# The opening of a fused DFT and gated feed-forward kernel: x laid out at partitions 0-46 and 64-110, its reversed halves loaded through ScalarE's queue, and the weight folds moved

## The chip, the cores and the metric

The program runs on one core of a Trainium2 chip. The metric is device microseconds from the start to the end of one execution. The profile is that of one more execution, with its own time; stamps count from the start of its span.

## What is computed

The reference takes x, eight sequences of 3008 tokens with 256 values each, and makes a two-dimensional Fourier transform of each (over the tokens and over the values), of which it keeps the real part. Each of the 24064 rows then goes through a small feed-forward layer: it is multiplied by a 256 x 2048 matrix, the result h becomes h cos(h), and that is multiplied by a 2048 x 256 matrix. All is float32.

```python
X = np.fft.fft(x, axis=1)
X = np.fft.fft(X, axis=2)
x = X.real.reshape(B * S, D)
h = x @ w_in
g = h * np.cos(h)
return g @ w_out
```

## The kernel before

The transform over 3008 = 47 x 64 tokens is split in two. A **first half** multiplies rows of x by a constant matrix L (the 47-point part); its result z goes through a scratch in DRAM, which changes the order of its axes, and comes back as z2. A **second half** multiplies z2 by the constants BJ (the 64-point part with the twiddle factors) and gives pq. The transform over the 256 values is never made by itself: it is folded into the first weight, WC and WS, by multiplying the constants CS with w_in (`weights`, L408) in four quarters of 512 columns. One row of each folded quarter is also turned into a column (`weight_row`, L428, then wn on ScalarE and a memset of that row on GpSimd, L442). `fold_quarter(n)` does all of this for a quarter: four matmuls of 512 columns, each in two passes, two copies from PSUM by ScalarE and the row.

Symmetry halves the work. Sequence index i (0 to 31) is paired with 64 - i, so x is loaded twice over: 47 rows forward and 47 rows with the index running backward. In the kernel before they lie at partitions 0-46 and 47-93 of a tile "xp". A tile holds eight values of i (a piece p of 0 to 3), and a piece is loaded by four transfers (six for p = 0): 32 rows and 15 rows, forward (L147) and reversed (L155; for p = 0 L150 and L151). The forward rows are 8 KB in one run each; the reversed ones are runs of 1 KB. For the first sequence (b = 0) VectorE folds the two halves of the 256 values together (`fold`, L227), while GpSimd copies two edge columns (L234); a chunk is half a piece, so there are eight chunks. Two buffers xf0 take the chunks in turn, so the fold of chunk c + 2 waits until TensorE has read chunk c. TensorE's `first_half` (L250 to L267) makes z of a chunk, ScalarE copies it out of PSUM (L279), and `store_z` (L317) and `load_z` (L327) take it through DRAM.

The order of every engine's instructions is written out by hand: instructions run on their engine in the order in which the program names them (`manual_schedule`). All DMAs but two at the very end are issued by SP (SyncE). DMAs take eight landing semaphores in turn. The order of the opening stands at L191 to L195 and L746 to L833: L, piece 0 of x, CS, weight quarter 0, piece 1; chunks 0 to 2, quarter 0 folded, two stores of z; weight quarter 1, pieces 2 and 3; chunks 3 and 4, quarter 1 folded, and so on; after chunk 7 the first part of z (columns of j 0 to 3) goes out and comes back while quarter 2 is folded and six passes of filler matmuls run (`keep_busy(3, "M", 256)`, L464); then come the later parts of z, quarter 3, w2, and the second half for the first group. The main loop, eight sequences by six groups by eight steps, follows at L835, and works on later sequences' first halves between its own matmuls.

Of the kernel before, what the change touches and what calls it, by code (L numbers as in the profile page):

```python
# [18 lines left out]
ND = 256  # L19
NDFF = 2048  # L20
N2 = 47
NJ = 24
NI = 32
IP = 4
# [8 lines left out]
def _consts():  # L33

    s2 = np.arange(N2)
    j = np.arange(NJ)
    th = 2.0 * np.pi * np.outer(s2, j) / N2
    thm = 2.0 * np.pi * np.outer(46 - s2, j) / N2  # L40
    thh = 2.0 * np.pi * np.outer(s2 + 0.5, j) / N2
    z = np.zeros((N2, NJ))
    pad = np.zeros((2 * N2, 16))

    def stack(a, b, c, d):
        m = np.block([[a, b], [c, d]]).reshape(2 * N2, 2, NJ).transpose(0, 2, 1)
        return np.concatenate([m.reshape(2 * N2, 2 * NJ), pad], axis=1)

    LE = stack(np.cos(th), -np.sin(th), np.cos(thm), -np.sin(thm))
    LO = stack(np.sin(th), np.cos(th), -np.sin(thm), -np.cos(thm))  # L50
    LE0 = stack(np.cos(th), z, z, np.cos(thh))
    LO0 = stack(np.sin(th), z, z, np.sin(thh))
    L = np.concatenate([LE, LO, LE0, LO0], axis=1)
    L = np.concatenate([L, np.zeros((128 - 2 * N2, 256))], axis=0)

    k2 = np.arange(64)
    i = np.arange(NI)
    B = np.zeros((128, NJ, 128))
    for jj in range(NJ):
        phi = 2.0 * np.pi * np.outer(i, 47 * k2 + jj) / SEQ  # L60
        blk = np.concatenate([np.cos(phi), np.sin(phi)], axis=0)
        blk[0] = 1.0
        blk[NI] = np.where(k2 % 2 == 0, 1.0, -1.0)
        blk = blk.reshape(2, 2, 16, 64)
        for half in range(2):
            for r in range(2):
                for e in range(2):
                    p = 64 * half + 32 * r + 16 * e
                    B[p : p + 16, jj, 64 * e : 64 * e + 64] = blk[r, half]

    c = np.arange(ND)
    d = np.arange(128)
    ang = 2.0 * np.pi * np.outer(c, d) / ND
    CS = np.concatenate([np.cos(ang), -np.sin(ang)], axis=1) / TWO_PI
    CS[:, 128] = np.where(c % 2 == 0, 1.0, -1.0) / TWO_PI
    return (
        L.astype(np.float32),
        B.reshape(128, NJ * 128).astype(np.float32),
        CS.astype(np.float32),
    )  # L80
# [28 lines left out]
def kernel(  # L109
# [22 lines left out]
    ctx.enter_context(tc.manual_schedule())  # L132


    xs = {}

    def take_x(b, p):
        xs[b, p] = spool.tile([128, XP * ND], FP, tag="xp", bufs=4, name="xp")

    def load_x(b, p):  # L140
        if (b, p) not in xs:
            take_x(b, p)
        xt = xs[b, p]
        xv = xt.rearrange("r (i d) -> r i d", d=ND)
        i0 = XP * p
        for r0, r1 in ((0, 32), (32, 47)):
            nc.sync.dma_start(out=xv[r0:r1], in_=x_r[b, r0:r1, i0 : i0 + XP, :])  # L147
            q0, q1 = N2 + r0, N2 + r1
            if p == 0:
                nc.sync.dma_start(out=xv[q0:q1, 0:1], in_=x_r[b, r0:r1, 32:33, :])  # L150
                nc.sync.dma_start(  # L151
                    out=xv[q0:q1, 1:XP], in_=x_r[b, r0:r1, 63 : 64 - XP : -1, :]
                )
            else:
                nc.sync.dma_start(  # L155
                    out=xv[q0:q1], in_=x_r[b, r0:r1, 64 - i0 : 64 - i0 - XP : -1, :]
                )

# [26 lines left out]
    def load_w2(f0, f1):  # L185
# [2 lines left out]
            in_=moe_w_out.rearrange("(q p) c -> p q c", p=128)[:, 2 * f0 : 2 * f1],  # L188
        )

    nc.sync.dma_start(out=L, in_=L_dr.ap())  # L191
    load_x(0, 0)
    load_cs()
    load_w(0)
    load_x(0, 1)  # L195
    WC = cpool.tile([128, NDFF], FP, tag="WC", name="WC")
    WS = cpool.tile([128, NDFF], FP, tag="WS", name="WS")
    wn = cpool.tile([128, 16], FP, tag="wn", name="wn")
# [19 lines left out]

    def fold(b, c, e):
        lo = IP * (c % 2)  # L220
        xv = xs[b, c // 2].rearrange("r (i d) -> r i d", d=ND)[0 : 2 * N2, lo : lo + IP]
        if b == 0:
            xfs[b, c] = xf0[c % 2]
        elif e == 0:
            xfs[b, c] = spool.tile([128, 2 * IP * 128], FP, tag="xf", bufs=2, name="xf")
        fv = xfs[b, c].rearrange("r (e i d) -> r e i d", e=2, d=128)[0 : 2 * N2]
        (nc.gpsimd if b else nc.vector).tensor_tensor(  # L227
            out=fv[:, e, :, 1:128],
            in0=xv[:, :, 1:128],
            in1=xv[:, :, 255:128:-1],  # L230
            op=ALU.subtract if e else ALU.add,
        )
        if e:
            (nc.scalar.copy if b else nc.gpsimd.tensor_copy)(  # L234
                out=fv[:, :, :, 0].rearrange("r e i -> r i e"), in_=xv[:, :, 0:129:128]
            )
# [2 lines left out]

    def first_half(b, c, pz=None):  # L240

        rows = 2 * N2 if b else 128
        fv = xfs.pop((b, c)).rearrange("r (e c) -> r e c", e=2)[0:rows]
        LE, LO, LE0, LO0 = (L[0:rows, 64 * q : 64 * q + 64] for q in range(4))
        pz = pz or psum("pz", "M")
        a = 128 if c == 0 else 0
        for e, (w, w0) in enumerate(((LE, LE0), (LO, LO0))):
            rows = slice(64 * e, 64 * e + 64)
            if a:
                nc.tensor.matmul(  # L250
                    pz[rows, 0:128], lhsT=w0, rhs=fv[:, e, 0:128], start=True, stop=True
                )
            nc.tensor.matmul(  # L253
                pz[rows, a:512],
                lhsT=w,
                rhs=fv[:, e, a:512],
                start=not a,
                stop=True,
                skip_group_check=True,
            )  # L260
        if b:
            return pz
        if a:
            nc.tensor.matmul(
                pz[64:128, 0:1], lhsT=LE0, rhs=fv[:, 1, 0:1], start=True, stop=True
            )
        nc.tensor.matmul(  # L267
            pz[64:128, a:512:128],
            lhsT=LE,
            rhs=fv[:, 1, a:512:128],  # L270
            start=True,
            stop=True,
        )
        keep_z(b, c, pz)
# [10 lines left out]
    zm = cpool.tile([128, NI], FP, tag="zm", name="zm")  # L285

    def take_middle(b, p):
        xv = xs[b, p].rearrange("r (i d) -> r i d", d=ND)[0 : 2 * N2]
        nc.scalar.copy(out=xm[0 : 2 * N2, XP * p : XP * p + XP], in_=xv[:, :, 128])

    def clear_middle():
        pm = borrow("pm", 1)[64:128, 0:NI]
# [3 lines left out]
    def middle(pm):  # L296
        for i0, i1, q in ((0, 1, 2), (1, NI, 0)):
            nc.tensor.matmul(  # L298
                pm[:, i0:i1],
                lhsT=L[0 : 2 * N2, 64 * q : 64 * q + 64],  # L300
                rhs=xm[0 : 2 * N2, i0:i1],
                start=False,
                stop=True,
                skip_group_check=True,
            )
# [1 line left out]
    zds = {}  # L307
    z2s = {}

    def store_z(b, c, j0=0, j1=NJ):  # L310
        half, q = divmod(c, NCH // 2)
        if q == 0 and j0 == 0:
            zds[b, half] = dpool.tile([32, 2 * NJ * 128], FP, tag="zd", bufs=4, name="zd")
        zd, zs = zds[b, half], zss[b, c]
        for e in range(2):
            p0 = 16 * e + IP * q
            nc.sync.dma_start(  # L317
                out=zd[p0 : p0 + IP, 256 * j0 : 256 * j1].rearrange("i (y d) -> y i d", d=128),
                in_=zs[64 * e + 2 * j0 : 64 * e + 2 * j1, :].rearrange("y (i d) -> y i d", d=128),
            )  # L320

    def load_z(b, half, j0=0, j1=NJ):
        if b not in z2s:
            z2s[b] = spool.tile([128, NJ * 128], FP, tag="z2", bufs=1, name="z2")
        for r in range(2):
            p0 = 64 * half + 32 * r
            nc.sync.dma_start(  # L327
                out=z2s[b][p0 : p0 + 32, 128 * j0 : 128 * j1].rearrange("i (j d) -> i j d", d=128),
                in_=zds[b, half].rearrange("i (j r d) -> r i j d", r=2, d=128)[r, :, j0:j1],
            )  # L330
# [123 lines left out]
    ones = cpool.tile([1, 128], FP, tag="ones", name="ones")  # L454
    nc.vector.memset(VX[:, 0:512], 1.0)
    nc.vector.memset(ones, 1.0)
    wrow = cpool.tile([1, 256], FP, tag="wrow", name="wrow")
    scratch = cpool.tile([1, 128], FP, tag="scratch", name="scratch")
    nc.scalar.activation(out=scratch, in_=ones, func=AF.Sin, bias=0.0, scale=SIN_SCALE / 8)
# [285 lines left out]

    keep_busy(2, "H", 512)  # L746
    keep_busy(2, "H", 512)
    chunk(0)
    chunk(1)
    first_half(0, 0)  # L750
# [4 lines left out]
    take_wn(0)  # L755
    store_z(0, 0, 0, 4)
    store_z(0, 1, 0, 4)
    load_w(1)
    load_x(0, 2)
    load_x(0, 3)  # L760
    chunk(3)
    first_half(0, 2)
    chunk(4)
    first_half(0, 3)
    fold_quarter(1)
    store_z(0, 2, 0, 4)
    store_z(0, 3, 0, 4)
    x1 = spool.tile([128, XP * ND], FP, tag="xp", bufs=4, name="wr")
    wr.append([x1[:, 1024 * i : 1024 * i + 1024] for i in range(2)])
    load_w(2)  # L770
    load_bj(0, 512)
    store_z(0, 0, 4)
    store_z(0, 1, 4)
    chunk(5)
    first_half(0, 4)
    chunk(6)
    first_half(0, 5)
    store_z(0, 4, 0, 4)
    store_z(0, 5, 0, 4)
    chunk(7)  # L780
    first_half(0, 6)
    first_half(0, 7)
    store_z(0, 6, 0, 4)
    store_z(0, 7, 0, 4)
    for half in range(2):
        load_z(0, half, 0, 4)
    fold_quarter(2)
    keep_busy(3, "M", 256)
    load_w(3)
    load_w2(0, 2)  # L790
    load_w2(2, 4)
    for c in range(2, 8):
        store_z(0, c, 4)
    load_bj(512, 1024)
    for half in range(2):
# [154 lines left out]
```

## Time and profile before

| what | us |
|---|---|
| median of the 3 runs shown | 1958.27 |
| lowest and highest of these | 1957.38, 1958.48 |
| the profiled execution's own time | 1957.18 |
| its span | 1955.4 |
| PE busy | 1940.8 |
| ScalarE (ACT), VectorE (DVE), GpSimd (POOL) busy | 1516.3, 1455.8, 1396.4 |

Landmarks of the opening, from the trace:

| event | us from the start of the span |
|---|---|
| filler matmuls at the start end | 7.58 |
| last transfer of piece 0 of x lands | 8.22 |
| first matmul of chunk 0 | 9.13 |
| weight quarter 0 has landed | 10.43 |
| piece 1 of x has landed | 14.73 |
| first matmul of chunk 2 | 16.54 |
| weight quarter 1 has landed | 18.85 |
| pieces 2 and 3 of x have landed | 22.47, 25.66 |
| matmuls of chunk 7 end | 29.45 |
| first part of z is back | 34.63 |
| first matmul of the second half (L341) | 35.38 |
| first matmul of the main loop (L517) | 37.26 |

How to read it: the page gives each engine's busy time; the chain of waits goes back from the last instruction to what released each one; the timeline lists instructions in order of time, with the start, the duration, the engine, the line, the tiles written and read, and in brackets the idle time before. An issue of a DMA appears under SPq or ACTq; the landing comes from the semaphore records. A matmul of float32 appears as two passes. The clock granted to TensorE stood at 0.999 of full in the mean.

### The profile page before, as it was taken

How to read it: one execution, taken by the hardware profiler on the slowest of the kernel's cores; microseconds unless marked ns; L12 is line 12 of the kernel's file. 1: busy time of each engine (PE TensorE's matmuls, PEld its weight loads, DVE VectorE, ACT ScalarE, POOL GpSimd, SP SyncE). 2: the span in 40 equal slices, each digit the busy share in tenths (PEclk: the TensorE clock that was granted, in tenths of full speed). 3: DMA queues.
4: the chain of work that ended last, by engine and by line, in shares of the span. 5: the costliest groups of instructions: out<-in, count | busy, mean ns of one | idle time of the engine just before them, and what ended most of it. 6: DMA issues, size and time to landing. Idle time of an engine off the chain costs nothing.

```text
span 1955.4 us, 29697 instructions
## 1 busy us (share of the span) xinstructions
PE 1940.8 (99%) x9262; PEld 1686.2 (86%) x9262; DVE 1455.8 (74%) x2529; ACT 1516.3 (78%) x3450; POOL 1396.4 (71%) x1593
## 2 busy tenths in 40 slices
PE   9999999999999999999999999999999999999998
PEld 4888888888988889888898888988889888898887
DVE  3767777777777777777777777777777777788886
ACT  3777778777787787877778787788777877778775
POOL 3777767787577876787667776687767777666775
PEclk9999999999999999999999999999999999999999
DMA  8511124011230223201241111411114111100001
GB/s 199 126 32 39 23 54 78 21 36 39 49 68 18 41 41 64 47 22 40 41 80 29 38 28 41 86 24 41 27 36 86 23 38 28 38 22 16 12 16 28
DMA packets 176690, 88.70 MB, mean 45 GB/s; under 512 B 103303, under 2 KB 173622, under 8 KB 174902
## 3 DMA queue, kind: packets, MB, share of 16 engines
q1 hardware_dynamic: 176374, 86.68, 21.5%
q8 instruction: 75, 1.23, 0.3%
q14 instruction: 81, 0.66, 0.1%
q10 hardware_dynamic: 160, 0.13, 0.0%
HBM read 49.50 MB, written 37.27 MB: 44 GB/s over the span
## 4 chain that ended last, share of the span: by engine, by line
PE 97%; DMA 1%; ACT 0%; DVE 0%; SPq 0%; issue 0%; POOL 0%; POOLq 0%; ACTq 0%
PE M L608 58%; PE H L517 33%; PE pz L253 3%; PE pb L341 2%; DMA xp<-in_x_dram 1%; PE pw L408 0%; DMA wr<-in_moe_w_in_dram 0%; DMA nb<-nd 0%; DMA nd<-pq 0%; PE pz L250 0%; PE pm L298 0%; PE pd L464 0%; DVE r L549 0%; ACT H L498 0%; ACT r L555 0%
## 5 line engine op out<-in xcount | busy, mean ns | idle before, releaser
L575 POOL TENSOR_TENSOR S<-r 128x512 f32<-128x512 f32 (+1 forms) x383 | 474.8, 1240 | 453.0 <-DVE r L559 408.1
L555 ACT ACTIVATE r<-r 128x512 f32<-128x512 f32 (+1 forms) x768 | 477.5, 622 | 257.4 <-DVE r L549 254.5
L549 DVE SCALAR_TENSOR_TENSOR r<-r,H 128x512 f32<-128x512 f32 (+1 forms) x768 | 518.9, 676 | 199.0 <-ACT r L545 174.6
L559 DVE SCALAR_TENSOR_TENSOR r<-H,r 128x512 f32<-128x512 f32 (+1 forms) x768 | 519.2, 676 | 132.5 <-ACT r L555 92.5
L608 PE MATMUL M<-S,VX 128*128 128x256 f32 (+1 forms) x2304 | 615.7, 376 | 0.0
L608 PEld LDWEIGHTS M<-S,VX 128*128 128x128 f32 x2304 | 435.8, 190 | 70.9 <-issue 22.7
L517 PE MATMUL H<-pq,WC 128*128 128x256 f32 (+1 forms) x1536 | 455.7, 378 | 3.1 <-ACT H L498 2.9
L517 PE MATMUL H<-pq,WS 128*128 128x256 f32 (+1 forms) x1536 | 451.5, 376 | 0.0
L545 ACT ACTIVATE r<-H 128x512 f32<-128x512 f32 (+1 forms) x768 | 447.6, 583 | 0.0
L533 DVE TENSOR_TENSOR H<-ew,H 128x256 f32<-128x256 f32 (+1 forms) x768 | 324.8, 423 | 140.5 <-PE H L517 81.6
L608 PE MATMUL M<-r,w 128*128 128x256 f32 (+1 forms) x1536 | 387.8, 375 | 0.0
L498 ACT ACTIVATE H<-nb,wn 128x256 f32<-128x256 f32 (+1 forms) x766 | 365.8, 478 | 2.7 <-DMA nb<-nd 1.3
L529 ACT ACTIVATE ew<-H 128x256 f32<-128x256 f32 (+1 forms) x768 | 287.3, 374 | 98.2 <-PE H L517 94.4
L608 PEld LDWEIGHTS M<-r,w 128*128 128x128 f32 x1536 | 300.4, 197 | 27.0
L517 PEld LDWEIGHTS H<-pq,WC 128*128 128x128 f32 x1536 | 279.3, 190 | 50.1 <-ACT H L498 18.0
L517 PEld LDWEIGHTS H<-pq,WS 128*128 128x128 f32 x1536 | 290.2, 190 | 33.3 <-ACT ew L529 1.1
L581 POOL TENSOR_TENSOR S<-S,r 128x256 f32<-128x256 f32 (+1 forms) x383 | 275.5, 719 | 30.0
L582 POOL TENSOR_TENSOR S<-r,S 128x256 f32<-128x256 f32 (+1 forms) x383 | 274.5, 717 | 30.0
L608 PE MATMUL M<-S,w 128*128 128x256 f32 (+1 forms) x768 | 225.4, 375 | 0.0
L608 PE MATMUL M<-r,VX 128*128 128x256 f32 (+1 forms) x768 | 225.4, 375 | 0.0
L608 PEld LDWEIGHTS M<-S,w 128*128 128x128 f32 x768 | 150.6, 196 | 14.5
L608 PEld LDWEIGHTS M<-r,VX 128*128 128x128 f32 x768 | 146.0, 190 | 14.4
(74 smaller groups left out, 925.9 us busy)
## 6 DMA issues: line engine op xcount, KB each, us to landing
out_dram<-ob SPq DMA_DIRECT2D x728, 32.0 KB
xp<-in_x_dram SPq DMA_DIRECT2D x56, 256.0 KB
zd<-zs SPq DMA_DIRECT2D x112, 96.0 KB
z<-zd SPq DMA_DIRECT2D x28, 384.0 KB
xp<-in_x_dram SPq DMA_DIRECT2D x56, 120.0 KB
nb<-nd SPq DMA_DIRECT2D x40, 128.0 KB
wr<-in_moe_w_in_dram SPq DMA_DIRECT2D x8, 256.0 KB
w<-in_moe_w_out_dram SPq DMA_DIRECT2D x4, 512.0 KB
```

What stands on the lines that cost most here:

```text
L498: nc.scalar.activation(out=h.H[:, 0:T], in_=s.nb[:, 0:T], func=AF.Copy, bias=0.25, scale=wn[:, f : f + 1])
L517: nc.tensor.matmul(h.H[:, 0:T], lhsT=W[:, 128 * f : 128 * f + 128], rhs=s.pq[:, e * T : e * T + T], start=False, stop=True, skip_group_che ...
L529: nc.scalar.mul(out=h.ew[:, 0:T], in_=h.H[:, 0:T], mul=2.0)
L533: nc.vector.tensor_tensor(out=h.H[:, T : 2 * T][:, ::-1], in0=h.ew[:, 0:T], in1=h.H[:, 0:T], op=ALU.subtract)
L545: nc.scalar.activation(out=r, in_=y, func=AF.Copy, bias=BIG, scale=1.0)
L549: nc.vector.scalar_tensor_tensor(out=r, in0=r, scalar=-BIG, in1=y, op0=ALU.add, op1=ALU.subtract)
L555: nc.scalar.activation(out=r, in_=r, func=AF.Sin, bias=0.0, scale=SIN_SCALE)
L559: nc.vector.scalar_tensor_tensor(out=r, in0=y, scalar=-0.25, in1=r, op0=ALU.add, op1=ALU.mult)
L575: tt(out=sv[:, 0:2], in0=qv[:, 1:2].to_broadcast([128, 2, T]), in1=qv[:, 0:4:3], op=ALU.subtract,)
L581: tt(out=sv[:, 2], in0=sv[:, 1], in1=gv[:, 0, 0], op=ALU.subtract)
L582: tt(out=sv[:, 3], in0=gv[:, 1, 0], in1=sv[:, 2], op=ALU.add)
L608: nc.tensor.matmul(acc[key][m // 2][:, 256 * (m % 2) : 256 * (m % 2) + T], lhsT=w, rhs=a, start=first, stop=s.fp == 7, skip_group_check=True,)
```

## The change

Rows of x now lie at partitions 0-46 and 64-110 of one fixed tile for each piece, and L has its rows moved to match. The gap between them must hold zeros, so each tile gets one memset of partitions 32 to 63, by GpSimd for pieces 0 and 2 and by VectorE for 1 and 3; the transfer of rows 32 to 46 comes behind it. Operands of later sequences have 111 partitions instead of 94. For the first sequence the reversed rows are issued by ScalarE, the forward ones by SP; for later ones all by SP.

The order of the opening changes: the first transfer of x goes ahead of L; pieces 1 to 3 follow directly behind weight quarter 0; quarters 1 and 2 and a part of BJ come after all of x. Chunks 3 to 7 follow each other without a weight quarter between them. Quarters 1 and 2 are folded after chunk 7, where quarter 2 and the filler stood. Half 0 of z is loaded once chunks 0 to 5 have been sent to the store, half 1 after chunk 7; of the last store and the last load one transfer each is issued by ScalarE. The later parts of z of chunks 0 and 1 join those of the others, behind w2. Quarters 2 and 3 of the weight lie in two "r" buffers instead of an "xp" buffer.

```diff
-    L = np.concatenate([L, np.zeros((128 - 2 * N2, 256))], axis=0)
+    pad = [np.zeros((n, 256)) for n in (XO - N2, 128 - XR)]
+    L = np.concatenate([L[:N2], pad[0], L[N2:], pad[1]], axis=0)
...
+    xs = [cpool.tile([128, XP * ND], FP, tag=f"xp{p}", name=f"xp{p}") for p in range(4)]
+
+    def clear_gap(eng, p):
+        eng.memset(xs[p][32:XO], 0.0)
+
+    def load_x(b, p, parts=(0, 1)):
+        xv = xs[p].rearrange("r (i d) -> r i d", d=ND)
         i0 = XP * p
-        for r0, r1 in ((0, 32), (32, 47)):
+        back = nc.sync if b else nc.scalar
+        for r0, r1 in [((0, 32), (32, 47))[i] for i in parts]:
             nc.sync.dma_start(out=xv[r0:r1], in_=x_r[b, r0:r1, i0 : i0 + XP, :])
-            q0, q1 = N2 + r0, N2 + r1
+            q0, q1 = XO + r0, XO + r1
             if p == 0:
-                nc.sync.dma_start(out=xv[q0:q1, 0:1], in_=x_r[b, r0:r1, 32:33, :])
+                back.dma_start(out=xv[q0:q1, 0:1], in_=x_r[b, r0:r1, 32:33, :])
...
+    load_x(0, 0, (0,))
     nc.sync.dma_start(out=L, in_=L_dr.ap())
-    load_x(0, 0)
+    clear_gap(nc.gpsimd, 0)
+    load_x(0, 0, (1,))
     load_cs()
     load_w(0)
-    load_x(0, 1)
...
     nc.vector.memset(VX[:, 0:512], 1.0)
     nc.vector.memset(ones, 1.0)
+    for p in (1, 2, 3):
+        clear_gap(nc.gpsimd if p == 2 else nc.vector, p)
+        load_x(0, p)
...
     keep_busy(2, "H", 512)
     keep_busy(2, "H", 512)
+    load_w(1)
+    load_bj(0, 512)
+    wr.append([spool.tile([128, 1024], FP, tag="r", bufs=4, name="wr") for i in range(2)])
+    load_w(2)
     chunk(0)
...
-    load_w(1)
-    load_x(0, 2)
-    load_x(0, 3)
     chunk(3)
     first_half(0, 2)
     chunk(4)
     first_half(0, 3)
-    fold_quarter(1)
     store_z(0, 2, 0, 4)
     store_z(0, 3, 0, 4)
-    x1 = spool.tile([128, XP * ND], FP, tag="xp", bufs=4, name="wr")
-    wr.append([x1[:, 1024 * i : 1024 * i + 1024] for i in range(2)])
-    load_w(2)
-    load_bj(0, 512)
-    store_z(0, 0, 4)
-    store_z(0, 1, 4)
...
     store_z(0, 5, 0, 4)
+    load_z(0, 0, 0, 4)
     chunk(7)
     first_half(0, 6)
+    store_z(0, 6, 0, 4)
     first_half(0, 7)
-    store_z(0, 6, 0, 4)
-    store_z(0, 7, 0, 4)
-    for half in range(2):
-        load_z(0, half, 0, 4)
+    store_z(0, 7, 0, 4, True)
+    load_z(0, 1, 0, 4, True)
+    fold_quarter(1)
     fold_quarter(2)
-    keep_busy(3, "M", 256)
     load_w(3)
     load_w2(0, 2)
     load_w2(2, 4)
-    for c in range(2, 8):
+    for c in range(8):
         store_z(0, c, 4)
```

The scratch activation that brings in the table of the sine (L459) stands behind the loop over pieces 1 to 3 in the order of ScalarE.

## The prediction

> **What bounds it now.** I read the page first, its chain of work that ended last:
>
> ```profile
> PE 97%; DMA 1%; ACT 0%; DVE 0%; SPq 0%; issue 0%; POOL 0%; POOLq 0%; ACTq 0%
> ```
>
> TensorE carries nearly the whole span. PE is busy 1940.8 of 1955.4 us, and the main loop has no room that this edit touches: what can change is the opening, before the loop's first matmul at 37.26. So next the chain of waits for 0 to 36 us:
>
> ```profile
> 3.52 4.70 DMA xp<-in_x_dram
> ...
> 8.37 0.72 POOL xf L234
> 9.13 0.43 PE pz L250 x2
> ...
> 13.71 5.15 DMA wr<-in_moe_w_in_dram
> 18.85 0.02 issue
> 18.87 6.79 DMA xp<-in_x_dram
> ...
> 29.45 3.63 PE pw L408 x8
> 33.08 0.98 PE pw L428 x8
> 34.06 1.49 PE pd L464 x6
> ```
>
> Start and duration in us. The opening hangs on x: the first pair of chunks (8.22, then the edge copy on POOL), a weight quarter and the last piece of x (18.87 to 25.66). After that come a weight quarter (4.61 with its row) and 1.49 of filler matmuls until z is back. Then the timeline of PE, because PE does other work while it "waits":
>
> ```profile
> 11.94 3.70 PE L408 MATMUL pw<-wr,CS 128*128 128x512 f32 x8
> 15.57 1.05 PE L428 MATMUL pw<-ones,WS 1*128 1x1 f32 x8
> 16.54 1.08 PE L253 MATMUL pz<-xf,L 128*64 128x512 f32 x4
> ...
> 18.95 3.70 PE L408 MATMUL pw<-wr,CS 128*128 128x512 f32 x8
> ...
> 28.26 1.13 PE L253 MATMUL pz<-xf,L 128*64 128x512 f32 x3
> ...
> 29.38 3.70 PE L408 MATMUL pw<-wr,CS 128*128 128x512 f32 x8
> ```
>
> PE is almost gapless from 9.13: the quarter at 18.95 fills the wait for the later chunks. So an earlier x gains only what PE really idles or fills with nothing: 1.55 us before 9.13 (7.58 to 9.13), some 0.6 between chunks (0.39 at 26.61, 0.19 at 17.88), the filler, and chunks that run slower than they must. That is at most about 4 us of 1957. Last, the windows:
>
> ```profile
> 18.90:25.70 6.80, 6.80 (x30) 3.60 (x28) 2.48 (x4) 2.50 (x5) 1.36 (x3) 1.00 0.93 177
> ...
> 37.00:40.00 3.00, 3.00 (x11) 1.64 (x10) 0.00 (x0) 0.91 (x3) 0.52 (x1) 1.00 0.96 327
> ```
>
> The last two numbers are the DMA share and GB/s. The engines are equally busy, yet x moves at 177 GB/s where a 128-partition weight moves at 327. Packet records agree: a 1 KB packet takes 89 ns (mean) in the first window and 48 in the second, an 8 KB packet of x 662 ns against 309 for the fastest.
>
> **The change, step by step.** Times are of the profiled execution (1957.18 with 1.78 outside its span); the median of the runs shown is 1.09 above it.
>
> *First x.* It now needs no turn behind six SP issues: ACT issues the reversed half beside SP. The second SP piece must wait for the gap memset on POOL. No row is a 32x2048 memset; two 64x1024 took 1.83 together, so I take 1.84 from 0.73, ending at 2.6 (bounds 0.9 and 3.7). That piece was issued at 2.58 before, so it loses nothing; SP's CS and weights stand behind it. It lands between 4.7 (the 2.13 that L took from issue) and 7.2 (as before); I take 6.5, since 0.88 MB at the 237 GB/s of 2 to 10.5 us end at 5.7. With the POOL copy (0.72) the first chunk is ready near 7.3, under the filler that ends at 7.58. So PE starts at 7.7 instead of 9.13. The other three gap memsets (DVE, some 1.9 each from 128x512 in 0.48; POOL 1.84) end by 6.3, before the folds need these engines; uncovered, each would delay chunk 0 by its length.
>
> *ACT's queue.* This takes the place of the wait removed. Landing records show eight semaphores used in turn, and an issue waits for the DMA eight places earlier: the first x piece landed at 5.16 and the issue behind it came at 5.18; then 6.53 and 6.55, 7.16 and 7.18. ACT's two stores at the end take places in the same rotation, so the two queues share it. Counted through the new order, ACT's last three issues wait for the second half of weight quarter 0 (place 11), the reversed piece 1 (13) and its small part (15). Behind them on ACT stand the table load (1.28), the scratch activation (0.31) and every z and weight copy; TensorE's weight row waits for these. Weight quarter 0 landed at 10.43; at the same place I expect 10.8 (9 with the rate of full-width DMA, 13 if ACT's bytes push in ahead). Three issues at 0.45 (SP 0.33 to 0.50; ACT's own two at the end 1.31 together, so 0.65) give 12.15, table and scratch 13.75, three copies at 0.55 give 15.4, the weight row 1.05: the third chunk starts at **16.5**, against 16.54. So the 1.4 us won at the start are lost here.
>
> *Chunks 2 to 7.* Without the quarter between, they follow each other. The second starts 1.33 later (17.88 less 16.54, the row's memset on POOL being in between), the others at the pace of VectorE's folds (2.48 for two chunks, 1.24 each; TensorE's part is 1.15), and the last takes 1.2: 16.5 + 1.33 + 4 x 1.24 + 1.2 = **24.0**. Chunk 6 is folded from 20.3; all of x, L, CS and quarter 0 are 4.0 MB, at 226 GB/s (1.54 MB of the last two pieces in 18.85 to 25.66) from 2.0 done at 19.7: just covered.
>
> *Quarters 1 and 2* are 4.61 each (29.38 to 33.99): **33.2**. Their weights, 1.05 MB behind x, land some 5 us after it, near 25, the second quarter being needed at 28.6. The z round trip took 4.6 us from copy to landing (30.06 to 34.63); from 24.6 it ends near 29.2, 4 us under cover. The filler goes. The two issues on ACT for z add a wait: ACT sits until the last store lands (1.44 from issue at 30.87 to 32.31), about 26.7, and then copies WS, which the weight row wants at 27.6. That fits by 0.3; uncovered it costs up to 1.
>
> *Second half* starts at 33.2 instead of 35.38: 2.2 us. All behind it moves along: quarter 3 and w2 are issued earlier relative to need (the loop's start is held by ACT and DVE latencies, 42 to 50). Sixteen late stores instead of twelve, 80 KB each, start about 6 us earlier and have 10 us to spare (z landed at 54.8, used at 65.2). PE's 0.78 us at 75.5, waiting for nb, may shrink; I count 0, bounds 0 and -0.8. From batch 1 on the operands have 111 partitions instead of 94 with unchanged free sizes. The by-shape rows of L253 give 603 ns on 94 rows and 615 on 128 for 512 columns, 486 on both for 384; I take 0, the upper bound being 196 x 0.012 = 2.4. The folds on POOL (1264 on 94 rows, 1240 for L575 on 128 rows of 512) show no price of rows either.
>
> *Two rules against these rows.* The Trainium skill, SBUF — State Buffer, section Door 1, says that DMA bandwidth follows the number of SBUF ports reached and that partition bit 6 picks the other half of the ports; the doubled packet times of x agree, and by it forward and reversed rows in flight together could run near 327 GB/s, which is the fast rival below. DMA: Bandwidth & Descriptors, section Issuing engines are not separate DMA queues, says that both queues run on the same 16 engines and save only issue time; that is the rival of unchanged bandwidth.
>
> Sum: 1957.18 - 2.2 = 1955.0, and 1.1 more on the scale of the median: **1956.1**.
>
> **Rivals.** *Full-width rate.* Were x at 300 GB/s or more, quarter 0 would land at 9.3, the third chunk start at 15.0, the second half at 31.7: 3.7 gained, with the nb wait 4.5, so 1953.8. For it: half-speed packets of x. Against: ACT still waits through its issues.
>
> *No more bandwidth.* At the 190 GB/s of the whole stretch before (4.5 MB from 2 to 25.7), x ends at 23.1; two folds and a chunk (2.48 + 1.2) give 26.8, the second half 36.0: 0.6 lost, 1958.9.
>
> *ACT starved (the slower side).* If the engines take one packet of each queue in turn, ACT's 1 KB packets (0.09) go between SP's 8 KB packets (0.65), and reversed rows fall behind. Per DMA engine these are 96 packets, and about as many on SP with the weights behind x; so the last reversed row lands with all 5.3 MB, 2 + 5.3/0.21 = 27. Then 27 + 2.48 + 1.2 + 9.2 = 39.9 and ACT, held until about 16 by piece 1, is late too: 4.5 lost, 1962.8. It decides from the point where the third chunk starts after 18.7 or x ends after 22.5. For it: no run here shows two loaded queues. Against: packet shares above 1.2 in single microseconds show that an engine overlaps packets.
>
> **How the numbers follow.** Forecast 0.42, full-width 0.28, no more bandwidth 0.14, starved 0.16. About 0.2% (3.9 us) is what a measurement of this kernel can tell from no change: faster 0.28, within 0.56, slower 0.16. The range leaves out part of the starved case and the end of the full-width one: 1953.4 to 1960.6; the forecast's own is 1954.6 to 1957.6.
>
> **What would show it.** The third chunk's matmuls at 16.5 with ACT idle up to about 13.7, waiting to issue; chunks 1.24 apart, ending at 24.0; two quarters back to back behind them; the second half at 33.2 without a wait for z. The forecast is wrong if ACT's last x issue comes after 14.4, if x lands after 21, or if a wait for quarter 1 or z shows on PE.

## The result, and the profile after

| what | before | after |
|---|---|---|
| median of 20 runs each, on the same chip | 1958.39 | 1961.65 |
| lowest and highest | 1957.37, 1959.51 | 1957.86, 1963.41 |
| profiled execution: own time | 1957.18 | 1962.98 |
| its span | 1955.4 | 1961.2 |
| its mean granted clock | 0.999 | 0.995 |

The ratio is 1.0015 [1.0008, 1.0022]: the changed kernel is 3.3 us slower, where 2.2 us faster was forecast, and the median lies above the range. The difference stays inside 0.2% and is still resolved, by the number of runs.

The profiled execution of after is one of its longest: the span grew by 5.8, the median by 3.3. What follows reads places from the profile and sizes from the medians.

The page's shares look as before, except that ScalarE now has one per cent of the chain:

```profile
PE 97%; ACT 1%; DMA 1%; DVE 0%; issue 0%; POOL 0%; ACTq 0%; SPq 0%; DVEq 0%; POOLq 0%
```

The chain of waits of after, in the opening (start and duration in us):

```profile
2.55 4.73 DMA xp<-in_x_dram
7.31 5.98 DMA xp<-in_x_dram
13.31 0.33 ACTq L156
13.67 1.28 ACT L464
...
15.28 0.94 ACT zs L281 x2
16.22 0.49 ACT WS L421
16.75 1.05 PE pw L430 x8
...
26.60 1.80 DMA zd<-zs
29.18 1.45 DMA zd<-zs
30.86 0.35 ACTq L329
31.24 0.59 ACT WS L421
31.88 1.86 PE pw L430 x8
```

The path goes through ScalarE's queue twice. Up to 13.64 it issues x, then it loads its table and makes two z copies before the weight copy that TensorE's row waits for. At 26.60 it issues a z store, at 30.86 a z load, and only then the next weight copy. The timeline of ScalarE shows both holds from the inside (the bracket is the idle time before, and what ended it):

```profile
2.77 10.87 ACTq L156 DMA_DIRECT2D xp<-in_x_dram  x6
13.67 1.28 ACT L464 ACT_TABLE_LOAD   x1 [13.67 <-DMA xp<-in_x_dram]
...
26.60 0.28 ACTq L319 DMA_DIRECT2D zd<-zs  x1
...
30.86 0.35 ACTq L329 DMA_DIRECT2D z<-zd  x1
31.24 0.58 ACT L421 COPY WS<-pw 128x512 f32<-128x512 f32 x1 [4.67 <-DMA zd<-zs]
```

And the timeline of PE shows what each hold costs there:

```profile
16.75 1.05 PE L430 MATMUL pw<-ones,WS 1*128 1x1 f32 x8 [1.42 <-ACT WS L421]
...
25.88 3.70 PE L410 MATMUL pw<-wr,CS 128*128 128x512 f32 x8
31.88 1.86 PE L430 MATMUL pw<-ones,WS 1*128 1x1 f32 x8 [2.30 <-ACT WS L421]
33.67 6.17 PE L410 MATMUL pw<-wr,CS 128*128 128x512 f32 x8
39.77 1.05 PE L430 MATMUL pw<-ones,WS 1*128 1x1 f32 x8
40.75 1.16 PE L343 MATMUL pb<-BJ,z 128*128 128x128 f32 x8
```

Two waits, 1.42 and 2.30. But look at the durations too. The same eight passes of a quarter's matmuls take 3.70 at 25.88 and 6.17 at 33.67, and the row 1.05 or 1.86. The windows tell why (stretch, length, busy time of PE, PEld, DVE, ACT and POOL, then granted clock, DMA share, GB/s):

```profile
15.30:17.70 2.40, 0.98 (x9) 0.95 (x8) 1.47 (x3) 1.87 (x4) 0.00 (x0) 1.00 1.04 176
17.70:21.20 3.50, 3.50 (x15) 1.55 (x16) 1.43 (x3) 1.04 (x3) 1.19 (x3) 0.57 1.05 193
...
29.60:31.90 2.30, 0.02 (x1) 0.02 (x1) 0.00 (x0) 0.66 (x2) 0.00 (x0) 0.99 0.11 22
31.90:38.60 6.70, 6.70 (x14) 3.95 (x15) 0.00 (x0) 1.17 (x3) 0.51 (x1) 0.50 0.91 271
...
55.40:59.20 3.80, 3.80 (x11) 3.45 (x12) 2.42 (x5) 2.67 (x6) 1.81 (x3) 0.55 1.04 338
```

Behind each wait the granted clock stands near half: 3.4 us from 18.2, 6.8 us from 31.8, and 3.4 us from 55.7, behind two waits at the start of the main loop. The kernel before has these two waits as well, there with the clock at full:

```profile
47.84 0.65 PE L517 MATMUL H<-pq,WC 128*128 128x225 f32 x2 [1.10 <-ACT H L498]
...
49.91 0.65 PE L517 MATMUL H<-pq,WC 128*128 128x225 f32 x2 [1.04 <-ACT H L498]
```

In after PE is busy in all three stretches; a busy PE at clocks of 0.57, 0.50 and 0.55 loses at most 1.5 + 3.4 + 1.7 = 6.6 us. That is more than the 5.8 by which the span grew.

From the one opening to the other: the first chunk starts 0.3 earlier (8.82 for 9.13), the third 1.2 later (17.73 for 16.54), the chunks last 8.15 from there to the first quarter, the quarters 7.8 and 7.1 instead of 4.6 each, and the filler is gone. So the second half starts at 40.75 instead of 35.38, and the loop's first M product 6.0 later (56.73 for 50.77). From there on the kernels run alike: from the start of the 101st to that of the last M matmul it is 1862.9 us before and 1862.6 after.

### The profile page after: what moved, and what is told of

Same layout as the page of the kernel before. It is cut to its first block, busy times and chain, and to the rows that moved or that the text cites. A ratio compares the mean times of both kernels' runs of the same rounds, so it can differ in the third digit from the quotient of the medians.

```text
span 1961.2 us, 29702 instructions
## 1 busy us (share of the span) xinstructions
PE 1943.6 (99%) x9256; PEld 1690.3 (86%) x9256; DVE 1459.4 (74%) x2531; ACT 1516.0 (77%) x3450; POOL 1399.9 (71%) x1595
## 4 chain that ended last, share of the span: by engine, by line
PE 97%; ACT 1%; DMA 1%; DVE 0%; issue 0%; POOL 0%; ACTq 0%; SPq 0%; DVEq 0%; POOLq 0%
PE M L613 58%; PE H L522 33%; PE pz L255 3%; PE pb L343 2%; DMA xp<-in_x_dram 1%; PE pw L410 0%; DVE r L554 0%; PE pw L430 0%; DMA zd<-zs 0%; ACT r L550 0%; ACT r L560 0%; PE pz L252 0%; PE pm L300 0%; POOL xp L141 0%; ACT H L503 0%
## 5 line engine op out<-in xcount | busy, mean ns | idle before, releaser
L580 POOL TENSOR_TENSOR S<-r 128x512 f32<-128x512 f32 (+1 forms) x383 | 474.9, 1240 | 453.1 <-DVE r L564 402.7
L613 PEld LDWEIGHTS M<-r,VX 128*128 128x128 f32 x768 | 146.4, 191 | 14.4
```

The source lines that it names most:

```text
L580: tt(out=sv[:, 0:2], in0=qv[:, 1:2].to_broadcast([128, 2, T]), in1=qv[:, 0:4:3], op=ALU.subtract,)
L613: nc.tensor.matmul(acc[key][m // 2][:, 256 * (m % 2) : 256 * (m % 2) + T], lhsT=w, rhs=a, start=first, stop=s.fp == 7, skip_group_check=True,)
```

## The experiments

Two things had to be told apart: what the holds of ScalarE cost as waits (and which part of the change makes them), and what the clock behind them costs. Later two more questions came up: a wait for nb that grew, and what the rows at 64 are worth. The medians, with the ratio to the kernel before on the same chip, the mean of the granted clock over a kernel's runs, and the start of the second half in its profile:

| kernel | median | ratio | clock | second half |
|---|---|---|---|---|
| before (33 runs beside the first four) | 1958.65 | 1 | 0.99785 | 35.38 |
| after | 1961.65 | 1.0015 [1.0008, 1.0022] | 0.99645 | 40.75 |
| e1_z_sp | 1957.70 | 0.9994 [0.9986, 1.0003] | 0.99700 | 35.72 |
| e2_x_sp | 1962.14 | 1.0015 [1.0006, 1.0024] | 0.99680 | 37.16 |
| e3_all_sp | 1957.75 | 0.9995 [0.9986, 1.0003] | 0.99800 | 34.75 |
| e4_layout | 1955.90 | 0.9986 [0.9977, 0.9995] | 0.99836 | 35.23 |
| e5_fill_holds | 1961.46 | 1.0011 [1.0003, 1.0020] | 0.99827 | 39.76 |
| e6_half_early | 1955.33 | 0.9982 [0.9974, 0.9991] | 0.99836 | 34.13 |
| e7_layout_fill | 1955.84 | 0.9985 [0.9976, 0.9994] | 0.99873 | 35.31 |
| e8_before_no_fill | 1959.83 | 1.0006 [0.9997, 1.0015] | 0.99764 | 35.75 |
| e9_all_sp_fill | 1955.25 | 0.9983 [0.9974, 0.9992] | 0.99891 | 35.11 |
| e10_fill_short | 1959.74 | 1.0004 [0.9995, 1.0013] | 0.99745 | 37.94 |
| e11_x_act_half | 1957.58 | 0.9992 [0.9983, 1.0001] | 0.99755 | 35.10 |
| e12_before_half | 1957.34 | 0.9995 [0.9986, 1.0004] | 0.99809 | 36.50 |
| e13_old_rows | 1957.67 | 0.9993 [0.9984, 1.0002] | 0.99818 | 35.27 |
| e14_layout_half | 1956.24 | 0.9986 [0.9977, 0.9995] | 0.99809 | 34.45 |
| e15_all_sp_old_rows | 1957.39 | 0.9989 [0.9980, 0.9998] | 0.99827 | 35.62 |

One run of e2, at 2540 us, is left out of its ratio and its clock; its median is 1962.14 with that run and 1962.12 without it. The kernels ran in four groups (e1 to e4, e5 to e8, e9 to e12, e13 to e15) on three chips, and before, which ran in each group, had medians from 1958.65 to 1959.08. Where kernels of different groups are compared, the ratios are the safer numbers.

**e1: the last z store and load issued by SP.** Against after:

```diff
-    store_z(0, 7, 0, 4, True)
-    load_z(0, 1, 0, 4, True)
+    store_z(0, 7, 0, 4)
+    load_z(0, 1, 0, 4)
```

> The changed kernel with the last z store and the last z load issued by SP alone; x stays on ACT for the first sequence. Theory A (ACT's instructions are held behind its own DMA issues, twice, and TensorE's clock falls in the waits): the second hold goes, so the WS copy of quarter 1 comes near 26.6 instead of 31.24, TensorE does not wait before the weight row, its clock stays at 1.00 from 26 to 40, and the second half starts at 35 to 36 instead of 40.75; the time falls by 3 to 5 us, to 1956.5 to 1958.5. Theory B (the transfers themselves come late, because all of x and three weight quarters stand ahead of z on the same DMA engines, and who issues does not matter): z is back at 33 or later as now, TensorE waits for z instead, and the time stays within 1 us of 1961.6. Theory C (111 partitions and the new layout cost time in the main loop): no change, 1961 to 1962.

Measured: 1957.70, some 4 us below after. PE's timeline shows that the second wait is gone:

```profile
26.50 3.70 PE L410 MATMUL pw<-wr,CS 128*128 128x512 f32 x8
30.13 1.05 PE L430 MATMUL pw<-ones,WS 1*128 1x1 f32 x8
```

The row follows its quarter without a bracket, the next quarter runs from 31.11 and the second half starts at 35.72, five us earlier than in the profile of after, where 6.8 us of half clock stand behind that wait. Two ACT issues for z cost that much because ScalarE copied no weights for the 4.67 us in which it waited to issue. Of the 4 us of the medians, the mean clock (0.99700 for 0.99645) is worth about 1.1; the rest goes with the wait.

**e2: the reversed x rows issued by SP, z still by ScalarE.**

```diff
-        back = nc.sync if b else nc.scalar
+        back = nc.sync
```

> The changed kernel with the reversed rows of x issued by SP also for the first sequence; the two z transfers stay on ACT. Theory A: ACT is free from the start, the first z copy comes as soon as chunk 0 is done (near 11.3 instead of 15.18), the weight row waits for nothing, the third chunk starts at 15.5 to 16.5 instead of 17.73, with the clock at 1.00; the second hold (until about 31) stays. So 1.5 to 3 us less than the changed kernel if the second hold does not absorb it, and 0 to 1.5 less if z comes back no earlier: 1959 to 1961.5. Theory B: the issues are more serial, x lands later, 1961.5 to 1963. Theory C: 1961 to 1962.

Measured: 1962.14, as slow as after. The first wait is gone, and nothing is won. ScalarE's store went out at 25.70 here, its load at 30.56 and the weight copy at 30.93, against 30.86 and 31.24 in after: the release of the second hold moved by 0.3 only. So the first hold lies under the second. The profile of this kernel shows no half clock in the opening, though PE waits 2.89 at 31.57. It is the fastest of its runs, 1957.66 at a mean clock of 0.999; the others that count stand at 0.996 and 0.997 and took 1960.8 to 1963.0.

**e3: both issued by SP.**

> The changed kernel with no DMA on ACT in the opening (both edits of the two kernels before). Theory A: neither hold; chunks end at 24 to 25.5, the two quarters follow without a wait at full clock, second half at 33.5 to 35, which is 0.5 to 2 us before the kernel before: 1956.4 to 1958. Theory B: second half held by z or x, 1960 to 1962. Theory C: 1961 to 1962.

Measured: 1957.75. The second half starts 0.63 earlier than before and the loop 0.55, but it is given back; the chain of waits of e3 shows where:

```profile
65.77 0.58 ACT pq L360
...
67.31 4.87 DMA nd<-pq
72.18 0.02 issue
72.19 4.04 DMA nb<-nd
76.26 0.49 ACT H L503
```

The row nb, one row of pq that goes through DRAM to all partitions and with which ScalarE starts the products of a group, is back at 76.24; PE waits 2.61 for it, where it waited 0.78 before. There the same trip reads:

```profile
66.94 3.83 DMA nd<-pq
70.76 0.02 issue
70.78 4.19 DMA nb<-nd
```

The loop comes sooner, the trip leaves 0.4 later and takes 0.9 longer.

Also, x is complete at 21.3 here and at 22.1 in after: one queue is no slower than two. The windows of 2 to 22 us, of after and then of e3:

```profile
2.00:22.00 20.00, 16.42 (x58) 7.59 (x58) 10.72 (x14) 5.12 (x10) 7.75 (x11) 0.91 1.05 217
```

```profile
2.00:22.00 20.00, 18.51 (x66) 8.36 (x64) 11.52 (x15) 5.46 (x12) 8.44 (x12) 1.00 1.01 231
```

**e4: the layout alone**, in the order of before, all issued by SP.

> The layout alone: rows at partitions 0-46 and 64-110, the gap memsets and 111-partition operands, with the order and the issuing engine of the kernel before. Theory A: the layout is free, 1957.9 to 1958.9, as the kernel before; the packets of x keep their doubled times, since forward and reversed rows still follow each other on one queue. Theory C: the layout carries the loss, 1960.5 to 1962.

Measured: 1955.90, faster than before by 2.7 [1.0, 4.5], and 5.7 below the whole change. The part that I had counted at nothing is the one that gains. This kernel keeps more of the change than the rows, though: x still has its fixed tiles, and the weights of quarters 2 and 3 their "r" buffers (e13 below takes the rows alone out again).

**e5: the holds kept, and filled.** Six passes of 512-column filler go before the row of quarter 0, ten before the row of quarter 1:

```diff
+    keep_busy(3, "H", 512)
     take_wn(0)
...
-    fold_quarter(1)
+    fold_weights(1, 1)
+    fold_weights(0, 1)
+    keep_busy(5, "M", 512)
+    take_wn(1)
```

> The changed kernel with filler matmuls where TensorE waits for ACT: three of 512 columns (1.39 us) ahead of the weight row of quarter 0, five (2.31 us) ahead of that of quarter 1. They replace idle time and take none of ACT's holds away. Theory D (the loss is the half clock that follows the waits, not the waits: a wait of 1.4 to 2.9 us inside one of the clock gate's stretches costs 3.4 us or more at half rate): the granted clock rises from 0.9965 in the mean to 0.998, the second half starts near 36.5 to 38 whenever a profile is taken, and the median falls by 2 to 3.5 us to 1958 to 1959.5. Theory A alone (ACT's hold itself, clock or no clock): the holds stay, so the median stays within 0.7 us of 1961.6.

Measured: 1961.46, for a plain reason that PE's timeline shows:

```profile
15.37 2.74 PE L469 MATMUL pd<-VX 128*128 128x512 f32 x6
...
29.78 4.45 PE L469 MATMUL pd<-VX 128*128 128x512 f32 x10
34.17 1.05 PE L430 MATMUL pw<-ones,WS 1*128 1x1 f32 x8
```

I had counted one pass for a filler matmul, and there are two. The rows came at 18.03 and 34.17, 1.3 and 2.3 later than in after; the 2.3 is what all behind them is late by. The clock rose from 0.99645 to 0.99827, worth 0.0018 x 1957 = 3.6. The two together would make it 1.3 faster than after; it is 0.2 faster at the medians, and the intervals overlap. So this kernel agrees with a cost of the clock, but doesn't show it.

**e10: the same with fillers that fit**, `keep_busy(2, "H", 256)` and `keep_busy(4, "M", 256)`.

> The changed kernel with fillers that fit into the waits: two of 256 columns (1.0 us) ahead of the weight row of quarter 0, four (2.0 us) ahead of that of quarter 1; the fillers before were of 512 columns and twice too long (2.74 and 4.45 us). Theory D: mean clock near 0.998 instead of 0.9965, no overrun, median 1958 to 1959.3. Theory A alone: 1961 to 1962.

Measured: 1959.74, 1.9 below after, with nothing released earlier: the rows start at 17.05 and 32.36, 0.3 and 0.5 later than in after. The clock rose by 0.0010, worth 2.0. Compare the windows with those of after, for the same stretches:

```profile
17.70:21.20 3.50, 3.31 (x20) 1.70 (x20) 2.04 (x4) 1.63 (x4) 1.80 (x4) 1.00 1.08 199
31.90:38.60 6.70, 6.37 (x30) 4.02 (x30) 0.00 (x0) 2.39 (x6) 0.98 (x2) 1.00 0.86 254
```

The clock is 1.00 in both, and in the second stretch PE ends 30 operations instead of 14. The time stayed a little above what the clock theory expected; the fillers leave waits of 0.73 and 0.33, and the runs' mean clock is still below that of before. The fillers do nothing for the two waits at the start of the loop, and in this profile 6.8 us at half clock begin there at 51.0:

```profile
52.00:55.40 3.40, 2.82 (x8) 2.56 (x9) 2.42 (x5) 2.30 (x7) 1.26 (x2) 0.50 1.13 276
```

**e8: before without its filler.** It takes `keep_busy(3, "M", 256)` out.

> The kernel before without the filler (six passes, 1.49 us) in front of the second half, which is otherwise the same; TensorE waits there for z. Theory D: in part of the runs the clock halves behind that wait: mean clock lower by 0.0005 to 0.001, median up by 0.5 to 2 us, spread wider, 1959 to 1960.5. Rival (a wait of 1.3 us is harmless, the clock only falls after the 2.3 to 2.9 us of the changed kernel): 1958.3 to 1958.9, no change.

Measured: 1959.83, 1.0006 [0.9997, 1.0015]: in the expected direction, but the interval takes in 1, and the clock fell by 0.0004 only. This tells little.

**e6: e3, and the second half of the next group one step earlier**, so that nb leaves sooner:

```diff
-        4: ((combine_w2, 4, 6, 2, 4),),
-        5: ((combine_w2, 6, 8, 0, 2), (second_half, 0, 1)),
+        4: ((combine_w2, 4, 6, 2, 4), (second_half, 0, 1)),
+        5: ((combine_w2, 6, 8, 0, 2),),
```

> The kernel with no DMA on ACT in the opening, and the second half of the second group one step earlier (step 4 instead of 5). Theory E (what the opening gains is given back at 75 us, where the seed of the second group waits for nb, whose way through DRAM stands behind the bulk transfers): the wait of 2.61 us there shrinks to 1 or less, and the median falls by 1 to 2.5 us below 1957.75, to 1955.3 to 1956.8. Rival: nb lands no earlier, since its transfers wait for the same landing places, and the wait only moves: 1957.2 to 1958.2.

Measured: 1955.33, 2.4 below e3 and 3.6 below before. No wait for nb is left on PE. With e3 this shows that an earlier opening is worth little as long as nb's trip does not move with it.

**e12 and e14: the same step in the order of before**, with the old layout and with the new one.

> The kernel before with the second half of the second group at step 4, nothing else. Theory E: its wait of 0.78 us for nb goes, in the runs where it is longer that too: 1957.3 to 1958.2 against 1958.4 to 1959.0 for the kernel before; the new order of the opening, all on SP, then has 2 to 3 us of its own. Rival: all of what the 1955.33 kernel gained comes from this step, 1955 to 1956.

> The layout alone in the order of before with the second half of the second group at step 4, without fillers. If the new order of the opening is worth something by itself, the 1955.33 kernel (new order, all on SP, same step 4) is faster than this one by 0.5 to 2 us, so this gives 1956 to 1957 at most as fast as 1955.9; if not, 1955 to 1955.6, and the reordering is worth nothing beyond the layout.

Measured: e12 1957.34, 1.3 below before, with an interval that takes in 1. e14 1956.24, no different from e4, which has no wait for nb to lose. Between e14 and e6, which differ in the new order alone, lie 0.9 us at the medians, with ratios of 0.9986 and 0.9982 whose intervals overlap. What the reordering is worth by itself, with all DMAs on SP, is thus not settled.

**e11: e6 with the reversed rows of x issued by ScalarE again.**

> Reversed rows of x on ACT as in the changed kernel, z on SP, second half of the second group at step 4: it differs from the 1955.33 kernel only in who issues the reversed rows. Theory A: the first hold costs its 1.4 us of wait, with a halved clock behind it in part of the runs: 1956.5 to 1958.5. Rival: the hold is absorbed by the later wait for the last x, 1955 to 1956.

Measured: 1957.58, 2.25 above e6. Here nothing covers the first hold: PE waits 1.49 at 16.77, the clock is at half for 3.4 us from 18.2, and the second half starts at 35.1 for 34.13. So the first hold costs about 2 us when the second does not hide it, as far as two medians can tell: the intervals of the ratios (0.9992 and 0.9982) overlap.

**e7 and e9: fillers in the two waits at the start of the loop**, on e4 with the earlier step and on e6. The diff is that of e9; e7 has 512 columns:

```diff
+        if k + 1 in range(4, AHEAD):
+            keep_busy(2, "M", 256)
```

> The layout alone in the order of before, with the second half of the second group one step earlier and two filler matmuls (0.92 us) in each of the two waits of 1.1 us at the loop's start (48 and 50 us). Theory D: the runs of the layout alone with a mean clock of 0.997 to 0.998 (5 of 11) disappear, the median falls from 1955.9 to 1955 to 1955.6 and the spread narrows. Rival (the fillers hold TensorE up, or the clock is not decided there): 1955.7 to 1957.

> The kernel with no DMA on ACT in the opening and the second half a step earlier (1955.33), with two filler matmuls of 256 columns (about 1.0 us) in each of the two waits of 1.1 us at the loop's start. Theory D: the runs with a mean clock of 0.997 and 0.998 (5 of 11) become rarer, the median falls by 0.3 to 0.8 to 1954.5 to 1955.1 and the spread narrows. Rival: the fillers only delay, 1955.3 to 1956.

Measured: e7 1955.84, e9 1955.25 (1954.29 to 1955.88). Neither median is below that of its kernel without fillers by more than the intervals. But ten of the eleven runs of e9 stand at a clock of 0.999 and one at 0.998; of e6 it is six, with three at 0.998 and two at 0.997 (1957.4 there, 1954.8 at 0.999). The fillers take away the runs at 0.997 and cost about as much as these did on average: the loop's first M matmul comes 1.0 later in the profile of e9 (50.61) than in that of e6 (49.63).

**e13 and e15: the reversed rows at 47 again**, without the memsets, in e4 and in e6 (`XO = N2`). These keep the fixed tiles and the "r" buffers.

> The layout-alone kernel with its rows put back to partitions 0-46 and 47-93 and without the gap memsets: what is left of the edit is the fixed tiles for x and the two r buffers for the weight quarters, in the order of before. Theory F (the new rows themselves are what made the layout alone 2.7 us faster, their packets in the loop taking 77 ns against 88 for 1 KB and 603 against 638 for 8 KB): 1958 to 1959, as the kernel before, with packets of 88 and 638. Rival (the fixed tiles, or the weights out of the x buffers, did it): 1955.5 to 1956.8.

> The 1955.33 kernel (new order, all on SP, step 4) with its rows put back to 0-46 and 47-93 and without the gap memsets. Theory F: x comes later by the longer packets and the loop's transfers too, 1956.5 to 1958; rival (the rows matter only in the old order): 1955 to 1956.

Measured: e13 1957.67, 1.8 above e4; e15 1957.39, 2.1 above e6. By the ratios it is 0.0007, or 1.4 us, in both pairs, and the intervals overlap. The 1 KB packets in the loop, most of them of x, take 75 to 76 ns (mean, from 100 us on) with rows at 64 (e4, e14, e6) and 87 to 90 with rows at 47 (before, e13, e15). But that is not where the time is: from the 101st to the last M matmul e13 takes 1862.3 us and e4 1862.2, e15 1862.0 and e6 1862.7. In e15 it is the opening. Two of its rows of PE:

```profile
19.75 1.81 PE L255 MATMUL pz<-xf,L 128*64 128x512 f32 x5 [1.20 <-POOL xf L236]
...
23.63 1.81 PE L255 MATMUL pz<-xf,L 128*64 128x512 f32 x5 [1.04 <-POOL xf L236]
```

The folds before them wait for x: they start at 18.92 and 22.80, in e6 at 17.80 and 21.32, where PE has one wait of 0.68. From 2 to 22 us e15 moves 206 GB/s and e6 236, and its second half starts 1.5 later. That accounts for most of e15. In e13 the opening is like that of e4 (35.27 and 35.23), and the profiles differ in one place, the second loop-start row. Here is e4 and then e13:

```profile
47.68 0.65 PE L522 MATMUL H<-pq,WC 128*128 128x225 f32 x2 [1.10 <-ACT H L503]
```

```profile
47.72 1.12 PE L522 MATMUL H<-pq,WC 128*128 128x225 f32 x2 [1.10 <-ACT H L503]
```

The wait is the same, and in e13 6.8 us at half clock begin there. But over all runs the clocks of e13 and e4 differ by 0.0002 (0.4 us), so this does not explain 1.4 to 1.8 us. Where the rest of it goes stays open, and so does whether there is a difference at all.

## Why the prediction was wrong, step by step

*First x.* Held in kind: the first chunk started at 8.82, before 9.13, instead of the 7.7 counted on. It waited for the last reversed part of piece 0, which ScalarE issued at 2.41 and which landed at 7.90, where 6.5 was counted for all of the piece.

*ScalarE's queue, first hold.* The mechanism was right, but the sum did not follow it. The prediction names a landing for each of the three last issues, and its sum then counts only the first, 10.8, and three issues behind it. In the run these issues, at 9.42, 11.12 and 13.31, came right behind the landings of CS (9.40), of the second half of weight quarter 0 (11.10) and of the reversed piece 1 (13.29), each one ScalarE issue earlier than counted. So the reversed piece 1, which was named there and not counted, ended the hold: the last issue ended at 13.64 for 12.15, and the third chunk started at 17.73 for 16.5. That last issue is still under the 14.4 from which I had called the forecast wrong. The term was mis-sized by 1.2, and it had a price that I had not seen: the clock, below.

*Bandwidth.* "At 226 GB/s ... done at 19.7": x was complete at 22.1, past the 21 that was to show the forecast wrong, and the stretch from 2 to 22 us had 217. The 226 put all of the last two pieces into the time from 18.85 on, though their transfers had been issued from 14.18 on; the window beside it has 177. All on SP it is 231 (e3), so the second queue carried nothing extra, and the rival "no more bandwidth" with its 23.1 was nearer for this term. The Trainium skill, DMA: Bandwidth & Descriptors, section Issuing engines are not separate DMA queues, says just this, and these traces agree. While forward and reversed rows were in flight together, from 11.6 to 21.2 us, the rate was 157 to 203, far from the 327 of the full-width rival. In the new order the rows at 64 went with a higher rate, 236 for 206 (e6, e15). By the Trainium skill, SBUF — State Buffer, section Door 1, all reversed rows now lie on the other half of the ports, where those at partitions 47 to 63 shared the half of the forward rows before. The packets of 75 to 76 ns for 87 to 90 agree in direction.

*The second hold: the step that failed.* "ACT sits until the last store lands ... about 26.7 ... That fits by 0.3; uncovered it costs up to 1." It sat until 31.24, and PE waited 2.30 for it. The 1.44 itself held: the last store took 1.45. What was wrong is when that store leaves. The 26.7 stands on an issue near 25.3, and it was issued at 29.18. Of these 3.9, 1.3 come from the later chunks (ScalarE's own store, right behind the last z copy, went out at 26.60), and 2.6 from the road of z on SP, which I had not followed:

```profile
20.39 6.51 SPq L319 DMA_DIRECT2D zd<-zs  x12
27.02 0.78 SPq L329 DMA_DIRECT2D z<-zd  x2
28.46 0.98 SPq L319 DMA_DIRECT2D zd<-zs  x3
30.83 0.31 SPq L329 DMA_DIRECT2D z<-zd  x1
```

The first z store, issued at 20.39 behind four weight transfers and BJ, landed at 25.21, where the last ones took 1.4 to 1.8. SP's eighth store waited for that landing and went out at 25.23. Then came the four of chunks 4 and 5, and the two loads of z's first half at 27.02 and 27.36; the store behind these waited for the landing place that ScalarE's own store (26.60) held until 28.40, and went out at 28.46. So the last store left at 29.18 and landed at 30.63, and ScalarE's load waits for it. With SP in its place (e1), the wait is gone.

*The clock: missing from the sum altogether.* A wait was priced at its length. In these kernels it costs its length, and in a part of the runs 3.4 or 6.8 us at half clock on top. At the medians: the mean clock fell from 0.99785 (before, the 33 runs beside e1 to e4) to 0.99645, worth 2.7 of the 3.3 us lost. Of after's own runs the two at 0.998 took 1957.86 and 1958.37, the four at 0.995 took 1963.1 (median); before at 0.998 takes 1958.5. At equal clock, as far as these two runs show, the change costs nothing, and gains almost nothing: the 2.2 forecast went into the second hold's 2.30. e1, without that hold, agrees: it is 1.0 faster than before at a clock 0.00085 lower, worth 1.7, so some 2.6 ahead but for the clock. e10 is the experiment for the clock: nearly the same release times, fillers in the waits, 0.0010 more clock, 1.9 us less. It fell short of what was expected of it, so the share is about right and not exact. One more reason for that: every profile ends at half clock, behind the last M matmul, for the last 3.4 to 6.1 us of its span (before, e7). That alone moves the mean clock of a run by up to 0.0007.

*The wait for nb* was counted 0, with bounds of 0 and -0.8. Where the second half did come earlier (e3), it grew from 0.78 to 2.61 and ate the gain: outside the bounds, on the wrong side. Without it (e6) the new order is faster than before.

*The layout* was counted 0, with a bound of +2.4. With the fixed tiles and the "r" buffers it is worth about -2.7 (e4). I looked for a price of 111 partitions in the matmuls, and the loop shows none (1862.2 in e4 for 1862.9); the 1240 set against 1264 for POOL was a mean over two shapes, and 128 rows of 512 alone have 1275. From the traces, e4 gains 0.15 up to the second half, 0.8 in the wait for nb and 0.7 in the loop; about 1.0 is clock (0.0005). How much of it is the rows' own stays open. The loop's 0.7 is not: e13 has it (1862.3) with the rows of before. The opening of e13 is that of e4, and its trip of nb can't be compared, since half clock delays the work ahead of it. At the medians e13 is 1.4 below before, with an interval that takes in 1.

*The rivals.* "ACT starved" gave 1962.8 and lies nearest to the result, but not by its mechanism: the reversed rows were not left behind (21.26, the forward ones 22.06), x did not end at 27, and neither of its two conditions came about (third chunk after 18.7, x after 22.5). The slow side came through ScalarE's second hold and the clock; that the number is near is luck.

## What to carry to other kernels

Here ScalarE, given DMAs to issue, stopped in its order until a landing place was free and the data's stores were back, for 10.87 us (with six issues in it) and for 4.67; follow that chain through every queue that it hangs on, with the durations under load, before trusting a margin of 0.3 us. Price a wait on TensorE by its length and by the half clock that may follow, and look at the clock of all runs, not of one profile. A gain at the front is kept only if the next thing late, here a trip through DRAM, is moved with it: e6, with the layout, all DMAs on SP and the second half one step earlier, is 3.6 us faster than before (0.9982 [0.9974, 0.9991]) and some 6 faster than the change as made.

## What the runs showed of the hardware

Ahead of the end of the span, half clock came in stretches of 3.4 and 6.8 us. It came behind the wait of 1.42 us in after (PE was busy 0.98 of the 2.40 us from 15.3 to 17.7), and behind a single one of 1.10 us: in e13 it begins at 47.8, where PE had been busy for 2.31 of the last 3.41 us. Whether a given wait is followed by it differs between executions: e2's profile has 2.89 us of wait and full clock. Of the fifteen profiles with the loop's two waits unfilled, seven have half clock there (after, e1, e5, e10, e12, e13, e14) and eight pass at full clock; the two with fillers there (e7, e9) have none. The Trainium skill, TensorE: Matmul & The Clock Gate, section Part 1: The HAM clock gate, gives a free-running window of 3413 ns; the lengths agree with one and two of these. The same page of the Trainium skill, section Why this matters for your kernels, advises against idle gaps above some 3 us; in these traces a gap of 1.10 us was enough, in a part of the executions.
